# Two groups of tokens without the seven-product scheme, and router dot products that read PSUM

## The chip, the cores and the metric

The kernel runs on one core of a Trainium2 chip. The metric is the device time of the core in microseconds. A core has five engines with a queue of instructions each: TensorE (PE, matmuls; its weight loads are listed as PEld), VectorE (DVE), ScalarE (ACT), GpSimd (POOL) and SyncE (SP, which issues most DMAs here). TensorE writes its sums to PSUM, eight banks of 128 x 512 float32; the other data lie in SBUF.

## The reference

Four steps, all in float32 (`w_in` and `w_out` come as float64). For 8 x 576 = 4608 tokens:

```
attention: k, v pooled by 8 along the sequence; softmax(q k_p^T / 8) v_p, 8 heads of 64  -> x (4608 x 512)
dense:     h = x @ w_in (512 x 2048);  g = h * sigmoid(h);  x2 = g @ w_out (2048 x 512)
router:    skip = x2 @ w_skip;  logits = x2 @ w_gate (512 x 8);  e = argmax;  p = softmax(logits)[e]
experts:   tokens with skip > 0: out = x2 + p * relu(x2 @ w1[e]) @ w2[e];  the others: out = x2
```

## The kernel before

A float32 product is made of three matmuls of a rounded type (fp32r): every operand is split into a high part (a cast, on ScalarE) and a low part (operand minus high part, on VectorE or GpSimd), and high x high, high x low and low x high are summed in PSUM. So each split costs an instruction on ScalarE and one on VectorE or GpSimd.

**First product.** The tokens are taken in NS = 9 groups of 512, the 2048 hidden columns in NP = 8 pairs of two 128-column blocks. For each group and pair (number n = 8 s + p) the 2 x 2 blocks (two halves of the tokens, two of the inner dimension, two column blocks) are multiplied by Strassen and Winograd's scheme: seven block products (`product`, L433, six matmuls of 256 columns each, 42 in all) in place of eight. For this, four differences of the x quarters per group (`x_diff`, L403), seven x operands split per group in place of four (`x_hi` L415, `x_lo` L419), four sums of the weight blocks per pair, made once (`w_sums`, L238), and seven weight operands split (`w_hi` L249, `w_lo` L253). Of the seven products three are copied out of PSUM (`keep`, L445) and three more are added to these in SBUF (`total`, L449). Then silu is applied by `tanh` (L455) and `swish` (L459): in three of four blocks both operands of `swish` lie in SBUF, in the fourth one of them is PSUM. `g_store` (L464) writes g of a pair, 512 KB, to DRAM.

Ahead of that the weights are converted from float64 by integer operations: `conv_abs`, `conv_low` (ScalarE, L215, L220), `conv_mix`, `conv_or` (VectorE, L224, L229). The attention of a group (L346 to L395) runs beside the products of the group before. The operands of x lie in a ring of ten places; three of these places lie where the conversion buffers were, and can be used only when all weights are converted and summed.

**Second product and router.** 18 chunks of 256 tokens. g is loaded again (L482), split (`g_hi` L490 on ScalarE, `g_lo` L494 mostly on GpSimd) and multiplied (`mm2`, L505 to L507, 96 matmuls of 512 columns a chunk). Each of the two 128-token tiles of a chunk has its sum in a PSUM bank; the banks are 4 and 5 for even chunks, 6 and 7 for odd ones. `evac` (L514, ScalarE) copies a tile to SBUF with the factor 0.5, and from there nine dot products per tile (`dot`, L524, VectorE: a multiplication of 128 x 512 with a row of the router's weights, summed along the row) give the eight logits and the skip score. For all chunks but the last, `route_a` (L537 to L545) makes a one-hot table, two small matmuls on TensorE (`route_sum`, L552 and L553) count the tokens in front, and `route_gate` and `route_place` compute the places to which GpSimd scatters the tokens' rows (L588). These two matmuls stand in TensorE's queue amid the matmuls of the next chunk.

**Order.** Everything up to here is an operation with a cost per engine, its predecessors and the buffers it takes (`op` in `dense`). `schedule` plays the operations through by these costs, takes the engine with the earliest end where there is a choice (with the additions `FIRST`, `LATER`, `KEEP`), and writes the instructions in this order into the engines' queues. `BONUS` shifts the priority by kind and stage. `SHARED` names the VectorE operations that it lets wait for a GpSimd operation under way. At run time each queue keeps its order and waits by semaphores.

**Experts.** Token lists per expert, gathers, and two products each (L1310 to L1382), with an order written by hand.

Of the kernel before, what the change touches and what calls it, by code (L numbers as in the profile page):

```python
# [40 lines left out]
NP = NF // 2  # L41
BONUS = {
    "w": {0: -1071.7, 1: -3755.8}, "abs": {0: 73.8, 1: 863.5}, "low": {0: -1795.5, 1: 3678.9},
    "mix": {0: 475.3, 1: -8181.9}, "or": {0: 1638.6, 1: -2069}, "ws": {0: 3059.3}, "wh": {0: 450.5},
    "wl": {0: -2429.5}, "vh": {0: 5650.7}, "vl": {0: 1208.1}, "k": {0: 2715.6, 1: 3293.7, 2: -1435.3},
    "ksum": {0: 571.4}, "kput": {0: -412.3, 1: -509.7, 2: -202.1}, "v": {0: 1646.8, 1: -131.2, 2: -136.6},
    "vsum": {0: -167.3, 1: -2320.7, 2: -6962.5}, "vput": {0: -645}, "clear": {0: 1916.3},
# [15 lines left out]
    "pset": {0: 614.5}, "blank": {0: 3833.5}, "router": {0: 1355.7}, "ft": {0: -103.1}, "fi": {0: -958.4},  # L63
    "l1": {0: 2010.1}, "l2": {0: 3836.1}, "ga": {0: 4003.4}, "ti": {0: -589.9}, "tc": {0: -1820.8},
    "xp": {0: -1226.1}, "xq": {0: 3529.9}, "xr": {0: 1345}, "s1h": {0: 2372}, "s1l": {0: -3330.5},
    "s2h": {0: -4085.4}, "s2l": {0: 395.6}
# [13 lines left out]
def body(tc, const, q, k, v, w_in, w_out, w_skip, w_gate, w_r, w1, w2, out, x2d, lst, gd, base, nch):  # L80
# [3 lines left out]
    with ExitStack() as ctx:  # L84
# [155 lines left out]
        PARTS = ((0, 512), (512, 768), (768, 1280), (1280, 1792))  # L240

        def w_part(p, k):
            src = cx_t[0, 2 * p + k % 2]
            lo, hi = PARTS[k]
            return src[:, 512 - (hi - lo):512], [w[:, p * 1792 + lo:p * 1792 + hi] for w in w7]
# [153 lines left out]
        HOME = (0, 2, 3, 0, 3, 1, 2)  # L399
# [5 lines left out]
        TURN = (0, 1, 4, 5, 3, 2, 6)  # L405

        def x_op(s, k):
            n = (7 * s + TURN.index(k)) % 10
# [8 lines left out]
        def x_lo(eng, s, k):  # L417
# [3 lines left out]
        WITH = {1: (0, 0, "b"), 2: (1, 1, "a"), 3: (4, 2, "b"), 4: (2, 6, "c"), 5: (6, 3, "b"), 6: (3, 4, "b"),  # L421
                7: (5, 5, "c")}

        def product(n, m, ps):
# [5 lines left out]
            for kk in range(2):  # L430
                for a, b in ((wh, xh), (wh, xl), (wl, xh)):
                    first, end = not on and kk == 0 and b is xh and a is wh, kk == 1 and a is wl
                    nc.tensor.matmul(out=ps, lhsT=a[:, kk], rhs=b[:, kk], start=first, stop=end, skip_group_check=on)  # L433

# [164 lines left out]
        def dense():  # L599
# [4 lines left out]
            def phase(kind, a=0, *_):  # L604
                if kind in ("q", "at", "sc", "mx", "ex", "ns", "nr", "pt", "pc", "pv", "xc"):
                    return min(a // 4, 2) if a < 4 * NS - 4 else 9
                if kind in ("mm", "cp", "ad", "th", "sw", "sv", "gs"):
                    return min(a // NP, 1) if a < NN - NP else 9
                if kind in ("xd", "xh", "xl", "w", "abs", "low", "mix", "or"):
                    return min(a, 1)  # L610
# [4 lines left out]
                if kind == "dot":  # L615
                    return 0 if a // TPC < nch - 2 else 8
# [14 lines left out]
            for late in range(2):  # L631
                order = f_order(1 - late)
                for f, old in zip(order, (None, *order)):
# [3 lines left out]
                    last["cx", c] = [("vl", f)] if late else [("wh", f // 2, f % 2 + 2), ("wl", f // 2, f % 2 + 2)]  # L637
# [977 lines left out]
```

## Time and profile before

Three runs took 1408.83 to 1412.42 us, median 1409.28. The profiled execution took 1409.15 us; its span, from the first to the last instruction in the trace, is 1407.4 us, at a mean granted clock of 0.951.

| engine | busy us | share of the span | instructions |
|---|---|---|---|
| TensorE, matmuls | 1256.0 | 89% | 8068 |
| TensorE, weight loads | 1115.9 | 79% | 8068 |
| VectorE | 1034.5 | 74% | 2459 |
| ScalarE | 648.5 | 46% | 1787 |
| GpSimd | 419.5 | 30% | 401 |

Busy time is the union of an engine's instructions in the trace; those of TensorE overlap one another, so a mean duration of a matmul is longer than the distance from one to the next. [...] A wait is put down to the instruction whose end released it. The shares are means over stages that differ.

### The profile page before, as it was taken

What the parts mean: (1) busy time and instruction counts of PE and PEld (TensorE: products, weight loads), DVE (VectorE), ACT (ScalarE), POOL (GpSimd) and SP (SyncE); (2) the same over time, 40 slices, a digit from 0 to 9 for tenths busy, and PEclk for the clock granted to TensorE, in tenths of its full rate; (3) what the DMA queues carried; (4) which work ended last, traced back from release to release, by engine and by line L of the source; (5) the groups of instructions that cost most, each with busy time, mean ns of one, the idle gap of its engine ahead of it and who ended that gap; (6) DMA issues with size and microseconds to landing.
All of it is one profiled execution on the core that took longest, in us unless ns stands there. A gap on an engine that the chain in (4) does not pass through costs nothing. (4 is left out here: it accounts for less than half of the span.)

```text
span 1407.4 us, 23981 instructions
## 1 busy us (share of the span) xinstructions
PE 1256.0 (89%) x8068; PEld 1115.9 (79%) x8068; DVE 1034.5 (74%) x2459; ACT 648.5 (46%) x1787; POOL 419.5 (30%) x401
## 2 busy tenths in 40 slices
PE   3578899999999998988887888788887999999998
PEld 2468899999999997867776677677767888888887
DVE  7999978878886789696887788868787445555462
ACT  5777777767777778322221222112223344444341
POOL 3553322020200000144454444445446111112211
PEclk9689999999999999998998999989998999999999
DMA  6354434344332357633433343324341554444541
GB/s 222 121 166 132 142 139 155 129 140 160 128 123 94 125 191 258 245 105 103 137 105 105 96 136 113 105 90 138 113 165 36 179 164 162 158 154 152 197 155 46
DMA packets 83030, 196.54 MB, mean 140 GB/s; under 512 B 14599, under 2 KB 15623, under 8 KB 82752
## 3 DMA queue, kind: packets, MB, share of 16 engines
q1 hardware_dynamic: 77008, 180.28, 38.6%
q0 software_dynamic: 5872, 14.44, 3.2%
q8 instruction: 71, 1.16, 0.3%
q14 instruction: 79, 0.65, 0.1%
HBM read 175.47 MB, written 64.36 MB: 170 GB/s over the span
## 5 line engine op out<-in xcount | busy, mean ns | idle before, releaser
L524 DVE SCALAR_TENSOR_TENSOR room<-xs,room 128x512 bf16<-128x512 f32 x306 | 307.6, 1005 | 84.0 <-ACT xs L514 72.6
L433 PE MATMUL bk<-ra,w7h 128*128 128x256 f32 x1440 | 271.4, 287 | 17.0 <-ACT outs L445 10.5
L494 POOL TENSOR_TENSOR w7l<-outs,w7h 128x512 fp32r<-128x512 f32 x129 | 187.7, 1456 | 304.0 <-ACT w7h L490 302.4
L433 PEld LDWEIGHTS bk<-ra,w7h 128*128 128x128 f32 x1440 | 225.7, 193 | 21.8 <-ACT outs L445 13.6
L490 ACT CAST w7h<-outs 128x512 fp32r<-128x512 f32 x144 | 89.2, 621 | 251.6 <-PE bk L506 248.5
L433 PE MATMUL bk<-ra,w7l 128*128 128x256 f32 x720 | 204.0, 283 | 0.0
L505 PE MATMUL bk<-w7h 128*128 128x512 f32 x468 | 198.9, 425 | 5.7 <-ACT w7h L490 5.7
L506 PE MATMUL bk<-w7l,w7h 128*128 128x512 f32 x468 | 194.8, 416 | 0.0
L507 PE MATMUL bk<-w7h,w7l 128*128 128x512 f32 x468 | 194.1, 415 | 0.0
L433 PEld LDWEIGHTS bk<-ra,w7l 128*128 128x128 f32 x720 | 138.4, 192 | 0.0
L505 PEld LDWEIGHTS bk<-w7h 128*128 128x128 f32 x468 | 95.8, 205 | 26.6 <-ACT w7h L490 6.3
L449 DVE TENSOR_TENSOR outs<-outs,bk 128x256 f32<-128x256 f32 x216 | 89.5, 417 | 34.0 <-PE bk L433 14.6
L507 PEld LDWEIGHTS bk<-w7h,w7l 128*128 128x128 f32 x468 | 95.7, 204 | 22.6 <-DVE w7l L494 0.9
L506 PEld LDWEIGHTS bk<-w7l,w7h 128*128 128x128 f32 x468 | 96.6, 206 | 20.5
L433 PE MATMUL bk<-rb,w7h 128*128 128x256 f32 x576 | 109.3, 284 | 1.9 <-DVE rb L419 1.8
L1311 PE MATMUL p<-w7l,w7h 128*128 128x256 f32 x352 | 101.0, 287 | 5.9 <-DVE w7l L1296 5.9
L455 ACT ACTIVATE t<-outs 128x256 f32<-128x256 f32 x216 | 89.6, 425 | 36.1 <-DVE outs L449 26.7
L1310 PE MATMUL p<-w7h 128*128 128x256 f32 x352 | 101.2, 288 | 3.1 <-PEq L1550 1.7
L459 DVE SCALAR_TENSOR_TENSOR outs<-t,outs 128x256 f32<-128x256 f32 x216 | 93.5, 446 | 11.6 <-ACT t L455 10.2
L1382 POOL DMA_INDIRECT out_dram<-xs,room x27 | 29.0, 1074 | 244.3 <-DVE xs L1378 172.0
L1312 PE MATMUL p<-w7h,w7l 128*128 128x256 f32 x352 | 100.9, 287 | 0.0
L1314 DVE SCALAR_TENSOR_TENSOR w7l<-p,w7h 128x256 fp32r<-128x256 f32 x88 | 36.6, 423 | 86.9 <-ACT w7h L1313 68.5
(253 smaller groups left out, 2765.5 us busy)
## 6 DMA issues: line engine op xcount, KB each, us to landing
gd<-outs SPq DMA_DIRECT2D x72, 512.0 KB
outs<-gd SPq DMA_DIRECT2D x72, 512.0 KB
outs<-in_w_dram SPq DMA_DIRECT2D x56, 512.0 KB
late<-in_w_dram SPq DMA_DIRECT2D x52, 512.0 KB
room<-in_w_dram SPq DMA_DIRECT2D x48, 512.0 KB
room<-in_v_dram SPq DMA_DIRECT2D x64, 144.0 KB
room<-in_k_dram SPq DMA_DIRECT2D x32, 288.0 KB
room<-in_q_dram SPq DMA_DIRECT2D x36, 256.0 KB
```

The costliest lines, as they stand in the source:

```text
L433: nc.tensor.matmul(out=ps, lhsT=a[:, kk], rhs=b[:, kk], start=first, stop=end, skip_group_check=on)
L449: nc.vector.tensor_tensor(out=o, in0=o, in1=ps[:, 0:CH], op=ALU.add)
L455: nc.scalar.activation(out=t, in_=ps[:, 0:CH] if m == 3 else part_of(n, SUM[m]), func=ACTF.Tanh, scale=0.5)
L459: nc.vector.scalar_tensor_tensor(out=part_of(n, SUM.get(m, 3)), in0=t_t.pop((n, m)), scalar=1.0, in1=h, op0=ALU.add, op1=ALU.mult)
L494: eng.tensor_tensor(out=lo, in0=src, in1=hi.bitcast(F32), op=ALU.subtract)
L505: nc.tensor.matmul(out=ps, lhsT=gh[:, ts], rhs=vh, start=first, stop=False)
L506: nc.tensor.matmul(out=ps, lhsT=gh[:, ts], rhs=vl, start=False, stop=False)
L507: nc.tensor.matmul(out=ps, lhsT=gl[:, ts], rhs=vh, start=False, stop=end)
L524: nc.vector.scalar_tensor_tensor(out=junk, in0=x2_t[i], scalar=1.0, in1=wb[:, e * DM:e * DM + DM], op0=ALU.mult, op1=ALU.mult, accum_out=l ...
L1310: nc.tensor.matmul(out=ps, lhsT=W1h4[:, kk, m], rhs=xh[:, kk], start=(kk == 0), stop=False)
L1311: nc.tensor.matmul(out=ps, lhsT=W1h4[:, kk, m], rhs=xl[:, kk], start=False, stop=False)
L1312: nc.tensor.matmul(out=ps, lhsT=W1l4[:, kk, m], rhs=xh[:, kk], start=False, stop=(kk == KD - 1))
```

## The change

The first PLAIN = 2 groups (16 pairs) are multiplied by the plain sum: `whole`, for each of two token halves and two column blocks two block products in one PSUM bank, 12 matmuls, so 48 a pair. No differences of x, four x operands, no copies or additions out of PSUM; silu reads PSUM. The second token half of a pair comes LATE = 1 pair later, and g is stored in halves of 256 KB. The weight parts of the plain sum are split first. During the second group the weights are rebuilt from their two parts (`w_back`), their sums made (`w_sums`) and the other parts split, in five operations instead of four; the fifth takes the place of a part that the last plain products read. The groups behind run the seven products as before. In the router, `dot` reads the skip score (c = 0, the row that is listed as `dot`) from the SBUF copy as before and the other eight (now `dp`) from the PSUM tile with the factor 0.5; the PSUM bank is free when these are done, the SBUF copy when its store and the one dot are. `wc`, `ra`, `rg` and `rb` are added to `SHARED`; `dp` is not in it. All values of `BONUS` and of the engine choice are new.

```diff
+PLAIN = 2
+LATE = 1
 BONUS = {
...
         def out_slot(n):
-            n = n % 2 if n < NP else (n - NP + 2) % 4
+            n = (n - PLAIN * NP + 2) % 4
...
-        PARTS = ((0, 512), (512, 768), (768, 1280), (1280, 1792))
+        def w_back(eng, p):
+            for c in range(2):
+                o = p * 1792 + c * 512
+                t = cx_t[0, 2 * p + c] = nth("cx", cxs, 512, 4)
+                h, l = (w[:, o:o + 512].bitcast(F32) for w in w7)
+                eng.tensor_tensor(out=t, in0=h, in1=l, op=ALU.add)
+
+        PARTS = ((0, 0, 512, 0), (1, 0, 512, 512), (0, 0, 512, 1024), (1, 256, 512, 1536), (1, 0, 256, 512))
...
+        def x_slot(s, k):
+            n = 4 * s + PTURN.index(k) if s < PLAIN else 8 + 7 * (s - PLAIN) + TURN.index(k)
+            return n, (n % 7 if n < 8 else (7, 8, 9, 1, 2, 3, 4, 5, 6, 0)[(n - 8) % 10])
...
+        def half_store(n, t):
+            s, p = divmod(n, NP)
+            nc.sync.dma_start(out=gd[s][t, :, 2 * p:2 * p + 2].rearrange("p f n -> p (f n)"), in_=ot_t.pop((n, t)))
+
+        def whole(n, c, ps):
+            s, p = divmod(n, NP)
+            t, f = divmod(c, 2)
+            ps = ps[:, 0:CH]
+            for half, k in enumerate(((0, 1), (7, 2))[t]):
+                wh, wl = w_of(p, 2 * f + half)
+                xh, xl = (x.rearrange("p (k n) -> p k n", n=CH) for x in x_op(s, k))
+                for kk in range(2):
+                    for a, b in ((wh, xh), (wh, xl), (wl, xh)):
+                        first, end = half == kk == 0 and b is xh and a is wh, half == kk == 1 and a is wl
+                        nc.tensor.matmul(out=ps, lhsT=a[:, kk], rhs=b[:, kk], start=first, stop=end)
+
+        def whole_tanh(n, c, ps):
+            t = t_t[n, c] = t_p.tile([128, CH], F32, tag="t", name="t")
+            nc.scalar.activation(out=t, in_=ps[:, 0:CH], func=ACTF.Tanh, scale=0.5)
+
+        def whole_swish(n, c, ps):
+            t, f = divmod(c, 2)
+            ot_t[n, t] = outs[0][:, half_of(n, t) % 4 * 512:half_of(n, t) % 4 * 512 + 512]
+            nc.vector.scalar_tensor_tensor(out=ot_t[n, t][:, f * CH:f * CH + CH], in0=t_t.pop((n, c)), scalar=1.0,
+                                           in1=ps[:, 0:CH], op0=ALU.add, op1=ALU.mult)
...
         def dot(i, e):
             j, t = divmod(i, TPC)
-            nc.vector.scalar_tensor_tensor(out=junk, in0=x2_t[i], scalar=1.0, in1=wb[:, e * DM:e * DM + DM],
+            x, scale = (o_t[j][t], 0.5) if e else (x2_t[i], 1.0)
+            nc.vector.scalar_tensor_tensor(out=junk, in0=x, scalar=scale, in1=wb[:, e * DM:e * DM + DM],
                                            op0=ALU.mult, op1=ALU.mult, accum_out=lg_t[j][:, t, e:e + 1])
...
-                op(("ws", p), {"V": 1.36, "G": 2.76}, lambda e, p=p: w_sums(e, p), [(c, p, k) for c in ("wh", "wl") for k in range(2)])
+                op(("wc", p), {"V": 1.2, "G": 2.46}, lambda e, p=p: w_back(e, p), [("wl", p, 0), ("wl", p, 1), ("wc", p - 1) if p else ("or", 0, f_order(1)[-1])],
+                   [("cx", ("cb", p, c)) for c in range(2)])
+                op(("ws", p), {"V": 1.36, "G": 2.76}, lambda e, p=p: w_sums(e, p), [("wc", p)])
+                for k in range(5):
+                    ca, cv, cg = (0.31, 0.34, 0.69) if k > 2 else (0.52, 0.6, 1.23)
+                    d = [("ws", p) if k > 1 else ("or", 0, 2 * p + k)]
+                    if k == 4:
+                        d += [("pl", (PLAIN - 1) * NP + p, c) for c in (1, 3)]
...
+                    free = [u for n0, slot0, u in used if slot0 == slot and n0 < n][-1:]
+                    if slot > 6 and not free:
+                        free = [[("wl", p, c) for p in range(NP) for c in range(2, 5)]]
...
+                for i, cs in ((n, (0, 1)), (n - LATE, (2, 3))):
...
+                        op(prev, {"T": 1.41}, lambda e, i=i, c=c: whole(i, c, bk["pl", i, c]), deps, [B(prev)])
+                        op(("th", i, c), {"A": 0.27}, lambda e, i=i, c=c: whole_tanh(i, c, bk["pl", i, c]), [prev] + old, [("t", ("t", i, c))])
+                        op(("sw", i, c), {"V": 0.34}, lambda e, i=i, c=c: whole_swish(i, c, bk["pl", i, c]), [("th", i, c)])
+                    op(halves[-1], {"S": 1.0}, lambda e, x=halves[-1][1:]: half_store(*x), [("sw", i, c) for c in cs])
...
-                    last["o", j, t] = [("ev", j, t)]
-                    dots = [("dot", i, c) for c in range(E + 1)] if j < nch - 1 else []
-                    last["x2", i] = dots + [("st", j, t)]
+                    dots = [("dp" if c else "dot", i, c) for c in range(E + 1)] if j < nch - 1 else []
+                    last["o", j, t] = [("ev", j, t), *dots[1:]]
+                    last["x2", i] = dots[:1] + [("st", j, t)]
...
-            SHARED = ("ns", "mix", "or", "wl", "ws", "vl", "xl", "xd", "sv", "nr", "vsum", "vput", "gl", "dot", "kput")
+            SHARED = ("ns", "mix", "or", "wl", "ws", "vl", "xl", "xd", "sv", "nr", "vsum", "vput", "gl", "dot", "kput", "wc", "ra", "rg",
+                      "rb")
...
-            FIRST = {"V": 1.472, "G": 0.36099, "A": -0.83284}
-            LATER = {"V": 5.6764, "G": 0, "A": -3.582}
-            FILL, HOLD, KEEP = 575.98, 0.9, 1.6007
+            FIRST = {"V": 6.8614, "G": -6.4915, "A": 6.2963}
+            LATER = {"V": -0.60269, "G": 0, "A": -3.3824}
+            FILL, HOLD, KEEP = -724.38, 1.0, -7.6842
```

## Rows read from the trace of the kernel before

**Rows 1.** Table of stages: start:end, length, busy us and count per engine, clock, DMA.
```profile
0.00:48.40 48.40, 20.58 (x104) 16.87 (x105) 37.47 (x72) 28.11 (x87) 21.21 (x36) 0.87 0.61 198
48.40:150.10 101.70, 74.74 (x587) 67.55 (x586) 97.69 (x202) 71.87 (x243) 46.43 (x53) 0.84 0.43 141
150.10:204.50 54.40, 52.58 (x472) 50.74 (x473) 43.69 (x117) 40.07 (x143) 12.42 (x19) 1.00 0.40 139
204.50:256.50 52.00, 52.00 (x482) 50.83 (x481) 43.40 (x115) 38.46 (x141) 10.10 (x17) 1.00 0.44 148
...
584.50:606.40 21.90, 21.90 (x100) 17.94 (x98) 20.24 (x54) 6.35 (x13) 5.73 (x4) 1.00 0.43 143
...
606.40:1035.60 429.20, 361.93 (x1474) 293.23 (x1473) 340.35 (x905) 91.33 (x166) 206.15 (x154) 0.91 0.34 110
...
413.60:466.30 52.70, 52.35 (x491) 50.64 (x490) 38.23 (x109) 38.62 (x140) 0.00 (x0) 1.00 0.26 96
```

**Rows 2.** The same table for the product matmuls, L433, alone (PE, PEld), third group.
```profile
204.50:256.50 52.00, 40.91 (x338) 40.14 (x337) 1.00 0.44 148
```

**Rows 3.** Instructions of the route sum's line, L552: durations, first and last start.
```profile
L552 PE MATMUL bk<-ohb,triu x17: 169/172/183, 606.3 to 1054.3; 128*128 128x16 bf16 x17
```

**Rows 4.** Waits from 606.3 to 1054.3 us: total us, times, longest.
```profile
PE bk L552 <- DVE ohb L545: 67.3, 15, 6.2
```

**Rows 5.** Instructions in order of time, one chunk: start us, duration us, engine, line.
```profile
694.74 0.69 DVE L524 SCALAR_TENSOR_TENSOR room<-xs,room 128x512 bf16<-128x512 f32 x1 [4.41 <-ACT xs L514]
695.31 1.29 POOL L494 TENSOR_TENSOR w7l<-outs,w7h 128x512 fp32r<-128x512 f32 x1 [0.29 <-ACT w7h L490]
695.47 1.67 DVE L524 SCALAR_TENSOR_TENSOR room<-xs,room 128x512 bf16<-128x512 f32 x1
...
710.68 0.39 PE L507 MATMUL bk<-w7h,w7l 128*128 128x512 f32 x1
...
712.49 0.69 DVE L524 SCALAR_TENSOR_TENSOR room<-xs,room 128x512 bf16<-128x512 f32 x1
...
713.22 0.69 DVE L524 SCALAR_TENSOR_TENSOR room<-xs,room 128x512 bf16<-128x512 f32 x1
...
715.39 0.17 PE L552 MATMUL bk<-ohb,triu 128*128 128x16 bf16 x1 [4.32 <-DVE ohb L545]
...
716.44 0.63 PE L507 MATMUL bk<-w7h,w7l 128*128 128x512 f32 x1
716.87 0.63 PE L505 MATMUL bk<-w7h 128*128 128x512 f32 x1
...
718.80 0.39 PE L507 MATMUL bk<-w7h,w7l 128*128 128x512 f32 x1
719.03 0.39 PE L505 MATMUL bk<-w7h 128*128 128x512 f32 x1
```

**Rows 6.** Groups of instructions, 606.4 to 1035.6 us: busy us, mean ns, idle before.
```profile
L524 DVE SCALAR_TENSOR_TENSOR room<-xs,room 128x512 bf16<-128x512 f32 x270 | 276.9, 1025 | 78.2 <-ACT xs L514 68.0 <-DVE room L524 0.5
```

**Rows 7.** Instructions in order of time in the first group, GpSimd and VectorE.
```profile
84.96 1.47 POOL L253 TENSOR_TENSOR w7l<-cxs,w7h 128x512 fp32r<-128x512 f32 x1
85.20 0.41 DVE L449 TENSOR_TENSOR outs<-outs,bk 128x256 f32<-128x256 f32 x1
...
86.38 1.83 DVE L459 SCALAR_TENSOR_TENSOR outs<-t,outs 128x256 f32<-128x256 f32 x2
86.39 1.53 POOL L308 TENSOR_TENSOR room<-room 72x512 f32<-72x512 f32 x1
```

**Rows 8.** Groups of VectorE's instructions, 413.6 to 466.3 us.
```profile
L459 DVE SCALAR_TENSOR_TENSOR outs<-t,outs 128x256 f32<-128x256 f32 x24 | 9.8, 422 | 2.3 <-ACT t L455 2.0
...
L459 DVE SCALAR_TENSOR_TENSOR outs<-t,bk 128x256 f32<-128x256 f32 x8 | 3.3, 412 | 0.0
```

**Rows 9.** Groups of VectorE's instructions in the first group, 48.4 to 150 us.
```profile
L238 DVE TENSOR_TENSOR cxs<-cxs 128x256 f32<-128x256 f32 x20 | 11.2, 559 | 0.5
L253 DVE TENSOR_TENSOR w7l<-cxs,w7h 128x512 fp32r<-128x512 f32 x13 | 11.1, 864 | 0.0
```

More of the change, by code (lines that the diff above doesn't have):

```diff
@@ L398, in body @@
         DIFF = {3: (0, 1, 0), 5: (1, 3, 1), 4: (3, 3, 0), 6: (2, 2, 3)}
-        HOME = (0, 2, 3, 0, 3, 1, 2)
+        HOME = (0, 2, 3, 0, 3, 1, 2, 1)
         def x_diff(eng, k):
@@ L636, in dense @@
                     last["sg", c] = [("or", *c)]
-                    last["cx", c] = [("vl", f)] if late else [("wh", f // 2, f % 2 + 2), ("wl", f // 2, f % 2 + 2)]
+                    last["cx", c] = [("vl", f)] if late else [("wh", f // 2, f % 2), ("wl", f // 2, f % 2)]
                     op(("w", *c), {"S": 1.95}, lambda e, c=c: load_w(*c), gone,
@@ new lines, in dense @@
+                for k in PTURN if s < PLAIN else range(7):
+                    n, slot = x_slot(s, k)
+                    free = [u for n0, slot0, u in used if slot0 == slot and n0 < n][-1:]
+                    if slot > 6 and not free:
+                        free = [[("wl", p, c) for p in range(NP) for c in range(2, 5)]]
+                    free = free[0] if free else []
+                    if s < PLAIN:
+                        used.append((n, slot, [("pl", s * NP + NP - 1, c) for c in ((0, 1) if k < 2 else (2, 3))]))
+                    else:
+                        used.append((n, slot, [("mm", s * NP + NP - 1, m) for m in WITH if WITH[m][1] == k]))
+                    used.sort(key=lambda x: x[0])
@@ L783, in dense @@
                     op(("xh", s, k), {"A": 0.52}, lambda e, s=s, k=k: x_hi(s, k), needs[k] + free)
                     op(("xl", s, k), {"V": 0.6, "G": 1.23}, lambda e, s=s, k=k: x_lo(e, s, k), [("xh", s, k)])
-            prev = None
-            for n in range(NN + 1):
+            prev, halves = None, []
+            for n in range(PLAIN * NP + LATE):
+                for i, cs in ((n, (0, 1)), (n - LATE, (2, 3))):
+                    if not 0 <= i < PLAIN * NP:
+                        continue
+                    s, p = divmod(i, NP)
+                    old = halves[-4:-3]
+                    halves.append(("gs", i, cs[0] // 2))
+                    for c in cs:
+                        deps = [prev, *[("xl", s, k) for k in ((0, 1), (7, 2))[c // 2]], s == 0 and ("wl", p, c % 2)]
+                        last["pl", i, c], last["t", i, c] = [("sw", i, c)], [("sw", i, c)]
+                        prev = ("pl", i, c)
+                        op(prev, {"T": 1.41}, lambda e, i=i, c=c: whole(i, c, bk["pl", i, c]), deps, [B(prev)])
+                        op(("th", i, c), {"A": 0.27}, lambda e, i=i, c=c: whole_tanh(i, c, bk["pl", i, c]), [prev] + old, [("t", ("t", i, c))])
+                        op(("sw", i, c), {"V": 0.34}, lambda e, i=i, c=c: whole_swish(i, c, bk["pl", i, c]), [("th", i, c)])
+                    op(halves[-1], {"S": 1.0}, lambda e, x=halves[-1][1:]: half_store(*x), [("sw", i, c) for c in cs])
@@ L788, in dense, with held @@
+            def held(n):
+                at = n - PLAIN * NP - 2
+                return [("gs", n - 4)] if at > 1 else halves[2 * at - 4:2 * at - 2 or None] if at >= 0 else []
+            for n in range(PLAIN * NP, NN + 1):
                 for d, m in ((0, 1), (0, 2), (1, 3), (0, 6), (1, 4), (0, 7), (0, 5)):
                     i = n - d
-                    if i < 0 or i == NN:
+                    if i < PLAIN * NP or i == NN:
                         continue
@@ L805, in dense @@
                     if m in (1, 6, 5):
-                        old = i - (2 if i < NP else 4)
                         op(("cp", i, m), {"A": 0.31}, lambda e, i=i, m=m, key=key: keep(i, m, bk[key]),
-                           [prev, m == 1 and old >= 0 and ("gs", old)])
+                           [prev] + (m == 1) * held(i))
                     if m in SUM:
@@ L819, in dense, with stored @@
                     op(("gs", n), {"S": 1.95}, lambda e, n=n: g_store(n), [("sw", n, 3)] + [("sv", n, m) for m in (2, 4, 7)])
+            def stored(j, a):
+                ns = [j // 2 * NP + 2 * a + c for c in range(2)]
+                return [("gs", n, j % 2) if n < PLAIN * NP else ("gs", n) for n in ns]
             for j in range(nch):
@@ L825, in dense @@
                     op(("ld", j, a), {"S": 1.95}, lambda e, j=j, a=a: g_load(j, a),
-                       old + [("gs", j // 2 * NP + 2 * a + c) for c in range(2)])
+                       old + stored(j, a))
                 for q, a in enumerate(blocks(j)):
@@ L845, in dense @@
                     op(("st", j, t), {"S": 1.95}, lambda e, i=i: store(i), [("ev", j, t)])
-                    for c in range(E + 1):
-                        if j < nch - 1:
-                            op(("dot", i, c), {"V": 0.72}, lambda e, i=i, c=c: dot(i, c), [("ev", j, t), ("router",)])
+                    for c, name in enumerate(dots):
+                        op(name, {"V": 0.73}, lambda e, i=i, c=c: dot(i, c), [dots[0] if c else ("ev", j, t), ("router",)])
                 if j == nch - 1:
@@ L852, in dense @@
                 op(("ra", j), {"V": 1.44}, lambda e, j=j: route_a(j),
-                   [("dot", TPC * j + t, c) for t in range(TPC) for c in range(E + 1)])
+                   [("dp" if c else "dot", TPC * j + t, c) for t in range(TPC) for c in range(E + 1)])
                 op(("rp", j), {"T": 0.06}, lambda e, j=j: route_sum(j, bk["rp", j]), [("ra", j)], [B(("rp", j), range(4))])
```

71 lines of the change are left out of this document (36 added, 35 removed), and 31 rows, old and new, of the table BONUS.

## Prediction

> **What bounds the kernel now.** I read the table of stages first, then the waits of the longest slow stage, then one chunk of it instruction by instruction, and last the durations of like instructions in other stages. The run has three stretches: the first dense product with the attention, the second dense product with the router, and the experts.
>
> In the table of stages TensorE is busy all of a full group, 52.00 of 52.00 us for eight pairs of 256 hidden columns plus the attention of the next group, at full granted clock. But the first group takes 101.7 us, the second 54.4, and the first product starts only at 48.4 us; there VectorE is busy 97.69 of 101.7 us and TensorE's granted clock is 0.84 [rows 1]. The row of the products alone confirms that this stretch is one group: 338 matmuls, where eight pairs of seven products of six make 336 [rows 2]. So the start, to 204.5 us, is VectorE's, and the seven groups behind it are TensorE's.
>
> The second dense product is neither engine's: from 606.4 to 1035.6 us TensorE is busy 362 of 429 us, VectorE 340, at clock 0.91. One chunk, 584.5 to 606.4, shows the pace without a stall: 21.90 us, all of it TensorE's, at clock 1.00 [rows 1]. The matmuls that sum the routes are a tick mark, one per chunk: 17 of them from 606.3 to 1054.3, so 448.0 / 16 = 28.0 us a chunk [rows 3]. That is 6.1 us a chunk over the pace, 16 x 6.1 = 97.6 us in all. The waits name it: TensorE stood 67.3 us in 15 waits before that matmul, for VectorE's one-hot table [rows 4].
>
> One chunk shows why. The 18 router dot products start at 694.74 us. One that runs alone takes 0.69 us and the next starts 0.73 later (712.49, 713.22). One that meets GpSimd's subtraction (1.29 us from 695.31) takes 1.67 us. TensorE finishes its product work ahead of the route sum at 710.68 + 0.23 = 710.91, and stands till 715.39. [...]
>
> **The dots from PSUM.** Eight of nine per tile, 16 of 18 per chunk, now read one operand from PSUM. The mean of a dot is 1.025 us there, against 0.69 alone [rows 5, 6]. What decides is whether a VectorE instruction with one PSUM operand still meets GpSimd. The early stage answers it. GpSimd runs L253 from 84.96 to 86.43; inside it VectorE's addition with a PSUM operand takes 0.41 us, no more than the swish of that size needs from PSUM where GpSimd does nothing, 0.41. The next GpSimd instruction starts at 86.39, and two swishes with both operands in SBUF need 1.83 us for what is 0.42 each alone [rows 1, 7, 8]. So I cost a PSUM dot at 0.73 us from start to start. 18 dots: 18 x 0.73 = 13.1 us from 694.74, so 707.9. The route arithmetic up to the matmul takes from the end of the last dot's slot, 713.22 + 0.73 = 713.95, to 715.39, 1.4 us, which makes 709.3, 1.6 us before TensorE comes to it. The two dots that still read SBUF can each meet GpSimd, 2 x 0.98 us late: 711.3, or 0.4 us of stall at the worst. The route arithmetic, now beside a GpSimd that no longer starves, may meet it once more (1 us). I take 0.6 us a chunk for stall and misplacement together, so 22.0 + 0.6 = 22.6 us a chunk and a gain of 16 x (28.0 - 22.6) = 86 us. Bounds: all of the 97.6 us, or nothing (and below nothing, as the last rival). Cover: VectorE was busy 340.35 us in this stretch of 15.3 chunks, 276.9 of it dots, so 4.1 us a chunk go to everything else [rows 1, 6]; 13.1 + 4.1 + 2 for the two meetings is 19.2, below 21.9 us, so TensorE bounds. The PSUM banks are held until the last dot, some 14 us longer; the bank pair is wanted again only two chunks on, 22 us after. Loads and stores move 110 GB/s here and would need 28.0 / 22.6 of it, 136 GB/s, less than the 198 of the first 48 us [rows 1].
>
> [...] The trace has the two forms of the swish side by side with GpSimd idle: 412 ns from PSUM, 422 from SBUF [rows 8]. By that I add nothing.
>
> **The plain sum in the first two groups.** TensorE: 48 matmuls of 256 columns a pair in place of 42, so 384 a group. At 40.91 / 338 = 0.121 us each [rows 2] a group's products take 46.5 us instead of 40.9; with the 52.0 - 40.9 = 11.1 us that attention has beside them, 57.6 us. From 48.4 us on two groups end at 163.6.
>
> VectorE, both groups together: gone are 3 additions x 16 pairs x 0.41 = 19.7 us, and of the x side 8 differences and 6 splits at the 0.86 us of a 128x512 tensor operation in this stage, 12.0 us. New are 16 additions that rebuild the weights from their two halves, 16 x 0.86 = 13.8, and 8 more splits of 256 columns at 0.56, 4.5 us [rows 8, 9]. Net -13.4 us of the 37.47 + 97.69 + 43.69 = 178.9 that VectorE spends up to 204.5 [rows 1]; 165.5 us at its present share of 0.96 end at 172. The sums of the weights (4 x 0.56 a pair) and three of the splits aren't saved but moved from the first group to the second; there VectorE was busy 43.69 of 54.4 us, and GpSimd, busy 12.42, can take a part [rows 1]. ScalarE loses 48 copies and 6 casts and gains 8 short ones; it was busy 71.87 of 101.7 us and does not bound.
>
> Moved past queues: the 512 KB store of a pair becomes two of 256 KB, so 16 more issues on SP, each of which can hold a weight load behind it until its swish is done. The stores go out one pair later for the second tile. I cost that at nothing; DMA moved 141 GB/s in the first group and weights are wanted faster, but 198 was reached before [rows 1].
>
> A new wait: the last weight part overwrites what the last plain products read, and the third group's first operand lies in the place of the conversion buffers, so cast, subtraction, cast, subtraction stand in a row between the last plain product and the next: about 0.4 + 0.6 + 0.6 + 0.7 and the hand-overs, an estimate of 4 us, and the attention of the next group can fill part of it. Queued behind it on TensorE is everything.
>
> Sum: between TensorE's 163.6 and VectorE's 172, plus 4 for that wait and 2 for two engines that both near their limit, 178 us in place of 204.5: -26 us. Bounds: -40 (TensorE alone bounds), and +16 (VectorE's saving is lost in the second group, and the 11.2 us of added matmuls and the wait stand).
>
> Everything else (seven full groups, the expert stage) I cost at nothing: the same instructions under the same bound. The whole planned order is new, which the rows cannot price.
>
> **Sum.** The profiled execution took 1409.15 us, 0.13 below the median 1409.28. 1409.15 - 86 - 26 = 1297.
>
> **Rivals.**
> Only the second product gains: the start gives its saving back, because the second group becomes VectorE's with 8 x (2 x 0.86 + 4 x 0.56 + 0.86 + 2 x 0.56) = 47.5 us of weight work beside its own. For it: VectorE is at 0.80 there already. Against it: the first group loses nearly as much. 1409 - 86 = 1323; with the whole +16, 1339.
> Only the start gains: dots from PSUM meet GpSimd as before, or another wait, such as GpSimd's low halves, takes the stall's place at the same 28 us. Against it: L449 inside L253 [rows 7], and GpSimd's waits are for ScalarE, which waits for TensorE. 1409 - 26 = 1383.
> Slower: a 128x512 dot from PSUM is itself slow while TensorE writes PSUM on every cycle, place VectorE between the tile's copy and the route sum. It decides from 1.025 + 26 / (16 x 16) = 1.13 us a dot on. At 1.18, half way between the short and the long dot, 16 x 16 x (1.18 - 1.025) = 40 us more: 1409 + 40 - 26 = 1423. Against it: every PSUM form in the rows is as short as its SBUF form, but at 256 columns only.
>
> **Chances.** Forecast 0.74 (own range 1270 to 1316), only the second product 0.15, only the start 0.07, slower 0.03, the rest 0.01 for no change. The range reaches from both gains in full, 1409 - 97.6 - 40 = 1271, to the first rival and most of its loss, 1335; I set 1268 to 1335. Within 0.3% is about what a measurement of this kernel can't tell from no change: 0.01. Slower 0.03, faster 0.96.
>
> **What would show it.** Right: the dots' mean falls to about 0.7 us with GpSimd's subtractions beside them; the wait of the route sum all but goes; route sums lie 22 to 23 us apart and the clock of that stretch is near 1.00. At the start, the third group's first product is near 178 us with a gap of a few us ahead of it. Wrong: dots above 0.9 us; a chunk still near 28 us with another releaser; the third group at 204 us or later; VectorE full and TensorE waiting in the second group.

## The result and the profile after

The changed kernel took 1283.66 us (median of 4 runs, 1282.66 to 1284.93), the kernel before 1409.37 beside it: a ratio of 0.9104, interval 0.9089 to 0.9120, some 126 us. The forecast was 1297, range 1268 to 1335. In the repeat of the changed kernel, the last of the experiments, one of six runs took 4255.83 us, and the numbers given for that repeat are those of the other five.

The span fell by 124.2 us, from 1407.4 to 1283.2. It is cut at the first matmul of the third group, at the first and the last matmul of the second product, and at the end:

| stretch | before, us | after, us | difference |
|---|---|---|---|
| start, two groups | 204.5 | 190.4 | -14.1 |
| groups three to nine | 350.8 | 354.0 | +3.2 |
| second product, router | 505.8 | 398.3 | -107.5 |
| experts | 346.4 | 340.4 | -6.0 |

The table of stages of the changed kernel, which answers to [rows 1]: start:end, length, busy us (and count) of TensorE, its weight loads, VectorE, ScalarE and GpSimd, granted clock (as a share of full speed), DMA share and GB/s. The first row is the lead-in up to the first product, the next two are the plain groups, the fourth the third group; the last three are the first chunk of the second product, the second chunk, and the 15 chunks behind them.
```profile
0.00:51.20 51.20, 26.60 (x136) 21.58 (x137) 37.93 (x74) 28.25 (x98) 11.05 (x24) 0.97 0.60 198
51.20:120.10 68.90, 65.47 (x570) 63.10 (x569) 64.46 (x140) 49.87 (x164) 19.07 (x23) 0.95 0.56 179
120.10:190.40 70.30, 64.20 (x554) 61.14 (x553) 62.61 (x146) 39.52 (x151) 29.49 (x40) 0.95 0.41 131
190.40:247.20 56.80, 54.17 (x480) 51.43 (x481) 45.98 (x119) 40.85 (x147) 11.11 (x17) 1.00 0.40 130
...
544.40:569.20 24.80, 23.84 (x97) 19.15 (x98) 16.11 (x27) 12.12 (x23) 0.00 (x0) 0.93 0.95 329
569.20:591.00 21.80, 21.80 (x99) 17.89 (x98) 18.91 (x58) 6.58 (x12) 0.00 (x0) 1.00 0.44 145
591.00:919.80 328.80, 328.80 (x1474) 270.05 (x1474) 273.44 (x964) 92.82 (x166) 114.38 (x95) 1.00 0.45 143
```
Two things are to be seen. In the last row TensorE is busy all of 328.80 us at clock 1.00, where it had 361.93 of 429.20 at 0.91: the second product is now TensorE's from its second chunk on. In the start the 102 and 54 us of the first two groups have become 69 and 70, and neither engine quite fills either of them.

The route sum's line in the changed kernel, the tick mark of [rows 3] (count, shortest, median and longest ns, first and last start), and what that line still waited for from 591.0 to 919.8 us, against [rows 4] (total us, times, longest):
```profile
L597 PE MATMUL bk<-ohb,triu x17: 182/183/184, 590.9 to 936.1; 128*128 128x16 bf16 x17
```
```profile
PEld L597 <- issue: 4.2, 16, 0.3
```
The ticks span 345.2 us where they spanned 448.0. The last row of the table holds 15 chunks (1474 matmuls) in 328.80 us, 21.9 us each; before, the same 1474 took 429.20 us [rows 1], 28.6 each. No wait of TensorE's matmuls for another engine is left in these chunks; 0.3 us a chunk of queue issue before the weight load is all.

VectorE's groups in the same 328.8 us (busy us, mean ns, then the idle time before them), against [rows 6]:
```profile
L569 DVE SCALAR_TENSOR_TENSOR room<-bk,room 128x512 bf16<-128x512 f32 x240 | 165.9, 691 | 8.3
L538 DVE TENSOR_TENSOR w7l<-outs,w7h 128x512 fp32r<-128x512 f32 x59 | 40.8, 691 | 15.7 <-ACT w7h L534 15.3 <-issue 0.3
L569 DVE SCALAR_TENSOR_TENSOR room<-xs,room 128x512 bf16<-128x512 f32 x30 | 20.7, 689 | 21.1 <-ACT xs L558 20.9
```
A dot takes 691 ns from PSUM and 689 from SBUF. The middle row was not forecast: 59 of the low halves of g (`g_lo`), which had nearly all been GpSimd's, are made by VectorE here. In the whole run GpSimd made 129 of the 144 before and makes 64 now; the new constants of the engine choice did that (with other constants, in an experiment below, GpSimd makes 134).

One chunk in order of time (start, duration, engine, line), against [rows 5]:
```profile
704.11 1.28 POOL L538 TENSOR_TENSOR w7l<-outs,w7h 128x512 fp32r<-128x512 f32 x1 [3.42 <-ACT w7h L534]
...
704.23 0.69 DVE L569 SCALAR_TENSOR_TENSOR room<-bk,room 128x512 bf16<-128x512 f32 x1
...
704.96 0.69 DVE L569 SCALAR_TENSOR_TENSOR room<-bk,room 128x512 bf16<-128x512 f32 x1
...
715.70 0.17 DVE L590 CAST ohb<-oh 128x16 bf16<-128x16 f32 x1
...
716.98 0.18 PE L597 MATMUL bk<-ohb,triu 128*128 128x16 bf16 x1
```
GpSimd's subtraction runs from 704.11 to 705.39, and the two dots beside it take 0.69 us and follow each other at 0.73. The one-hot table is ready at 715.87; TensorE comes to the route sum at 716.98. Where TensorE stood for 4.3 us [rows 5], VectorE is now 1.1 us ahead.

Of the start, four views say why it gained only 14 us. First VectorE's groups in the second plain group, 120.1 to 190.4 us, the three costliest:
```profile
L241 DVE TENSOR_TENSOR cxs<-cxs 128x256 f32<-128x256 f32 x24 | 14.7, 612 | 0.6
L476 DVE SCALAR_TENSOR_TENSOR outs<-t,bk 128x256 f32<-128x256 f32 x31 | 12.4, 412 | 5.8 <-ACT t L471 5.8
L248 DVE TENSOR_TENSOR cxs<-w7h,w7l 128x512 f32<-128x512 f32 x12 | 9.9, 865 | 0.0
```
Then a stretch of that group in order of time:
```profile
164.55 3.18 DVE L241 TENSOR_TENSOR cxs<-cxs 128x256 f32<-128x256 f32 x4
...
165.39 1.59 POOL L298 TENSOR_TENSOR room<-room 128x288 f32<-128x288 f32 x2
...
167.64 0.74 DVE L476 SCALAR_TENSOR_TENSOR outs<-t,bk 128x256 f32<-128x256 f32 x2
...
168.11 2.19 PE L356 MATMUL bk<-room 128*64 128x144 f32 x16 [2.80 <-DVE outs L476]
```
All that TensorE's matmuls waited for in the second group (us in total, times, longest):
```profile
PE bk L356 <- DVE outs L476: 2.8, 1, 2.8
PE bk L386 <- DVE outs L476: 1.8, 3, 0.9
PE bk L467 <- DVE outs L476: 0.2, 1, 0.2
```
And the boundary of the second and the third group on TensorE:
```profile
186.81 1.07 PE L386 MATMUL bk<-ident,room 128*72 128x128 f32 x8 [0.59 <-DVE outs L476]
187.81 1.25 PE L356 MATMUL bk<-room 128*128 128x144 f32 x8
190.45 0.50 PE L447 MATMUL bk<-rb,w7h 128*128 128x256 f32 x2 [1.39 <-DVE outs L476]
```
Four sums of weights (L241) with GpSimd beside them take 3.18 us on VectorE, two `swish` (L476) stand behind them in its queue, and TensorE waits 2.80 us for a PSUM bank that these free. All five waits of the group, 4.8 us together, end with a `swish`: what holds TensorE is VectorE's order of work, not one missing operand. The boundary itself costs two waits, one of these five (0.59 us) and one of 1.39 us.

### The profile page after: what moved, and what is told of

Read it like the earlier page. It is cut to its first block, busy times and chain, and to the rows that moved or that the text cites. A ratio compares the mean times of both kernels' runs of the same rounds, so it can differ in the third digit from the quotient of the medians.

```text
span 1283.2 us, 24162 instructions
## 1 busy us (share of the span) xinstructions
PE 1231.3 (96%) x8164; PEld 1103.6 (86%) x8164; DVE 946.9 (74%) x2506; ACT 633.3 (49%) x1741; POOL 288.5 (22%) x312
## 5 line engine op out<-in xcount | busy, mean ns | idle before, releaser
L447 PE MATMUL bk<-ra,w7h 128*128 128x256 f32 x1088 | 199.5, 283 | 1.1 <-ACT outs L489 0.7
L569 DVE SCALAR_TENSOR_TENSOR room<-bk,room 128x512 bf16<-128x512 f32 x272 | 188.0, 691 | 9.3
L447 PEld LDWEIGHTS bk<-ra,w7h 128*128 128x128 f32 x1088 | 166.8, 189 | 2.8 <-ACT outs L489 1.3
L447 PE MATMUL bk<-ra,w7l 128*128 128x256 f32 x544 | 152.5, 280 | 0.0
L538 POOL TENSOR_TENSOR w7l<-outs,w7h 128x512 fp32r<-128x512 f32 x64 | 82.3, 1290 | 102.9 <-ACT w7h L534 102.9
L447 PEld LDWEIGHTS bk<-ra,w7l 128*128 128x128 f32 x544 | 102.4, 188 | 0.0
L633 POOL DMA_INDIRECT lst<-row,du x36 | 40.5, 1125 | 266.6 <-DVE du L630 226.8
L1397 ACT ACTIVATE w7h<-p 128x256 fp32r<-128x256 f32 x88 | 33.5, 383 | 130.0 <-PE p L1396 130.0
L370 ACT ACTIVATE room<-bk,mx 128x72 f32<-128x72 f32 x288 | 88.8, 329 | 16.0 <-DVE mx L362 14.4
L467 PE MATMUL bk<-ra,w7h 128*128 128x256 f32 x512 | 96.0, 290 | 0.2 <-DVE outs L476 0.2
L447 PE MATMUL bk<-rb,w7h 128*128 128x256 f32 x480 | 91.3, 285 | 4.2 <-ACT outs L489 1.9
```

Source lines behind the costliest of these rows:

```text
L370: nc.scalar.activation(out=P_t[i][:, HP * g + h], in_=ps[:, h], func=ACTF.Exp, scale=esc, bias=mx[:, h], accum_out=sm_t[i][:, HP * g + h])
L538: eng.tensor_tensor(out=lo, in0=src, in1=hi.bitcast(F32), op=ALU.subtract)
L569: nc.vector.scalar_tensor_tensor(out=junk, in0=x, scalar=scale, in1=wb[:, e * DM:e * DM + DM], op0=ALU.mult, op1=ALU.mult, accum_out=lg_t[ ...
```

## The experiments

The account of the prediction for the second product: a dot with one operand in PSUM no longer meets GpSimd, and that alone is the gain. Its rival: the low halves that moved from GpSimd to VectorE removed the collisions, and PSUM has little to do with it. For the start: VectorE still bounds it; rivals are TensorE, the late second token half, and the hand-over at the boundary. A stage's times below are from the profiled execution of each kernel; ratios are to the kernel before, beside it on the same chip.

**The dots alone.** The kernel before, with eight of nine dots read out of PSUM and the PSUM bank held until they are done; start and engine choice as before, and the planned cost of a dot 0.73 us for 0.72. The line that reads x (the code that frees the bank and the SBUF copy is left out here):
```diff
-  in0=x2_t[i], scalar=1.0
+  x, scale = (o_t[j][t], 0.5) if e else (x2_t[i], 1.0)
+  in0=x, scalar=scale
```


> The kernel before with the dots from PSUM alone; first groups, priorities and engine choice as before. Theory A: dots 0.7 us, chunks near 22 us from the 28.0 of before, a gain of 85 to 105 us: 1304 to 1324 us. Theory B: most low halves stay on GpSimd and the order is the old one, so a gain under 40 us: over 1369 us.


Measured 1306.0 us, ratio 0.9268 [0.9229, 0.9306]: -103 us. The dots' group and the route sum's line of this kernel:
```profile
L525 DVE SCALAR_TENSOR_TENSOR room<-bk,room 128x512 bf16<-128x512 f32 x272 | 187.9, 691 | 9.3
```
```profile
L553 PE MATMUL bk<-ohb,triu x17: 169/183/184, 604.5 to 950.3; 128*128 128x16 bf16 x17
```
691 ns a dot and 345.8 us from the first tick to the last, with 129 of the low halves on GpSimd as before. The account holds and the rival is not needed.

**The dots back in SBUF.** The changed kernel, all nine dots from the SBUF copy; the bank is free again when the tile is copied (that code is left out here).
```diff
-  x, scale = (o_t[j][t], 0.5) if e else (x2_t[i], 1.0)
+  x, scale = x2_t[i], 1.0
```


> The changed kernel with all nine dots reading the SBUF copy again; costs, order rules and engine choice stay those of the changed kernel. Theory A (the PSUM operand keeps the dots out of GpSimd's way): about four low halves a chunk still run on GpSimd, each makes a dot about 1 us longer; dots' mean 0.85 to 1.0 us, chunks of 24 to 28 us where the changed kernel has 21.9, total 1315 to 1380 us. Theory B (the gain comes from moving over half of the low halves from GpSimd to VectorE and from the new order): chunks stay under 22.7 us, total under 1297 us.


Measured 1348.58, ratio 0.9564 [0.9523, 0.9604]: 65 us of the gain gone. Its dots, and TensorE's wait for the one-hot table (591 to 1000 us):
```profile
L569 DVE SCALAR_TENSOR_TENSOR room<-xs,room 128x512 bf16<-128x512 f32 x306 | 276.8, 905 | 33.0 <-ACT xs L558 23.7
```
```profile
PE bk L597 <- DVE ohb L590: 46.8, 16, 5.0
```
The dots are at 905 ns and the stall is back, but smaller than [rows 4] has it, since only 64 low halves are left on GpSimd. The dots' operand apart, TensorE, ScalarE and GpSimd run the same instructions in the same order as in the changed kernel, and so does VectorE but for 13 neighbouring pairs of small instructions (L613, L622), so another order did not make the difference.

**The low halves back on GpSimd.** The changed kernel with constants of the engine choice that give GpSimd 134 of the 144 low halves.
```diff
-  FIRST = {"V": 6.8614, "G": -6.4915, "A": 6.2963}
+  FIRST = {"V": -0.60269, "G": 0, "A": -3.3824}
-  LATER = {"V": -0.60269, "G": 0, "A": -3.3824}
-  FILL, HOLD, KEEP = -724.38, 1.0, -7.6842
+  LATER = {"V": 5.6764, "G": 0, "A": -3.3824}
+  FILL, HOLD, KEEP = 540.0, 1.0, 0.0
```


> The changed kernel with dots from PSUM, but the low halves of the second product priced off VectorE as in the kernel before, so that nearly all run on GpSimd. Theory A: dots stay at 0.69 us beside a GpSimd twice as busy, chunks about 22 us, total 1276 to 1294 us. Theory B: the stall before the route sum comes back, chunks of 25 us or more, total over 1330 us.


Measured 1287.12, ratio 0.9126 [0.9088, 0.9163], which can't be told from the changed kernel's. Its two groups:
```profile
L569 DVE SCALAR_TENSOR_TENSOR room<-bk,room 128x512 bf16<-128x512 f32 x272 | 187.9, 691 | 9.4
```
```profile
L538 POOL TENSOR_TENSOR w7l<-outs,w7h 128x512 fp32r<-128x512 f32 x134 | 174.6, 1304 | 247.2 <-ACT w7h L534 246.8
```
Twice as many GpSimd subtractions, and no dot from PSUM is longer.

**The start alone.** The two edits above together, so that of the change only the start is left.


> The changed kernel with both of the second product's parts undone: nine dots from SBUF and the low halves priced onto GpSimd as before, so the plain sum of the first groups stands alone. If the parts add as measured so far (third group's first product 190 us for 204.5, and some 4 us at the change to the second product), chunks are back at 27 to 29 us and the total is 1385 to 1398 us, a gain of 12 to 24 us. Rival (the start's gain was an effect of the new order as a whole): total 1400 us or more.


Measured 1391.03, ratio 0.9883 [0.9860, 0.9905]: -17 us, small but clear of 1. Its dots and the wait (591 to 1040 us):
```profile
L569 DVE SCALAR_TENSOR_TENSOR room<-xs,room 128x512 bf16<-128x512 f32 x306 | 310.7, 1015 | 87.7 <-ACT xs L558 76.5
```
```profile
PE bk L597 <- DVE ohb L590: 71.7, 17, 8.1
```
So the parts add up: -103 for the dots and -17 for the start are -120 of some -126. The low halves are worth some 42 to 45 us where dots read SBUF (1391.0 to 1348.6, or 0.9883 to 0.9564 by the ratios), and nothing that can be measured where they read PSUM. The rival names a real remedy, a second one for the same collision, which the first one makes idle.

**Without the weight sums.** The changed kernel with the instructions of `w_sums` left out, so the groups from the third on multiply wrong weights and the tokens are routed otherwise; what is compared is the start.
```diff
-  lambda e, p=p: w_sums(e, p)
+  lambda e, p=p: None
```


> The changed kernel without the four sums of weight blocks per pair (their instructions left out, so the products of the later groups use unsummed blocks; order and all else the same). Takes some 14 to 18 us of work off VectorE in the second group. Theory V (the second group, 70.3 us, is VectorE's, with the silu queued behind weight work): second group 60 to 64 us, total 1273 to 1278 us. Rival (the group is paced by TensorE's own 58 us, the attention chain and ScalarE): under 3 us, total 1280 to 1284 us.


The third group began at 180.4, 10.0 us earlier. The whole run, 1258.22 (ratio 0.8913), is no measure, for its expert stage is 13.5 us shorter with other tokens. Its second group, in the columns of the first table:
```profile
118.90:180.40 61.50, 61.14 (x555) 58.98 (x553) 52.51 (x122) 39.16 (x151) 29.76 (x40) 1.00 0.48 154
```
Ten us less on VectorE (52.5 for 62.6), and TensorE is busy 61.14 of 61.50 us at clock 1.00. With these 14.7 us of sums gone, the group is TensorE's. With them it is 8.8 us longer: TensorE is idle for 6.1 us of it instead of 0.4, and as many matmuls keep it busy for 3.1 us more, at clock 0.95 for 1.00.

**The weight work on GpSimd.** Twice: `w_back` on GpSimd alone, and `w_sums` on GpSimd alone.
```diff
-  op(("wc", p), {"V": 1.2, "G": 2.46}
+  op(("wc", p), {"G": 2.46}
```


> The changed kernel with the rebuilding of the weights (two additions a pair) allowed on GpSimd alone: 16 us off VectorE in the second group, some 22 us onto GpSimd. Theory V (VectorE's time in the second group sets its length): third group's first product at 180 to 186 us, total 1274 to 1280 us. Rival (longer GpSimd work holds VectorE's instructions with two SBUF operands, which are most of that group's weight work): third group at 188 us or later, total 1282 to 1292 us.


```diff
-  op(("ws", p), {"V": 1.36, "G": 2.76}
+  op(("ws", p), {"G": 2.76}
```


> The changed kernel with the four weight sums of a pair allowed on GpSimd alone: 18 us off VectorE in the second group, some 22 us onto GpSimd, in a chain of four for each pair. Theory V: third group at 180 to 187 us, total 1273 to 1281 us. Rival: third group at 188 us or later, total 1282 to 1295 us.


Measured 1291.6 (0.9181 [0.9157, 0.9206]) and 1288.99 (0.9162 [0.9139, 0.9184]): slower than the changed kernel. The third group began earlier, at 186.6 and 187.3, but its first pair took 15.46 and 12.38 us instead of 7.18, and the second product began at 547.9 and 545.7 instead of 544.5. TensorE at the boundary, with `w_back` on GpSimd:
```profile
186.58 0.35 PE L447 MATMUL bk<-rb,w7h 128*128 128x256 f32 x1 [3.66 <-POOL room L298]
...
193.72 0.58 PE L447 MATMUL bk<-rb,w7h 128*128 128x256 f32 x1 [3.92 <-ACT rb L429]
```
GpSimd is now late with the attention's own work (L298), and the x operands of the third group come after it. What was won is more than given back at the boundary. And less was won than was moved. `w_back` had been 15.5 us of VectorE and `w_sums` 18.1, but VectorE's busy time up to the third group fell only from 165.0 to 161.0 and 157.3 us, for other instructions of VectorE became longer beside a GpSimd that does more. The 28 scalings of the row maximum (4 columns each) went from 7.1 to 10.9 us in the first of the two runs, the 28 of the softmax sum from 7.0 to 9.7 in the second. Those that overlap no work of GpSimd took 173 ns at most, as before; what grew is the number and the time of the others. The rival of the first expectation had named this. Both totals lie in the rivals' ranges, but both starts of the third group lie between the ranges of the two theories.

**The second token half at once.** The changed kernel with no delay between a pair's halves.
```diff
-LATE = 1
+LATE = 0
```


> The changed kernel with LATE = 0: both token halves of a pair right after each other, so the very first pairs need all four tiles of the group's attention. First product of the first group's second half waits for tiles 2 and 3: first group longer by 2 to 8 us, total 1284 to 1294 us. If the attention is ahead anyway: within 2 us of the changed kernel.


Measured 1285.03, ratio 0.9125 [0.9101, 0.9150]: no difference from the changed kernel that these intervals show. The first product began at 45.5 us, nearly 6 earlier, and the third group at 192.3, 2 later. In this start, TensorE's beginning earlier did not bring the end forward.

**Taking small work off VectorE.** The changed kernel without the scaling of the softmax sum, a VectorE instruction on 4 columns per half tile; the factor goes into ScalarE's copy of x, and the added 1e-9 is left out. The planned order is the same.
```diff
-  nc.vector.tensor_scalar(out=sm, in0=sm, scalar1=1e-9, scalar2=float(POOL), op0=ALU.add, op1=ALU.mult)
-  nc.scalar.copy(out=x5[...], in_=ps...)
+  nc.scalar.activation(out=x5[...], in_=ps..., func=ACTF.Copy, scale=1.0 / POOL)
```


> The changed kernel in the same planned order, without the small scaling of the softmax sums (72 instructions of VectorE on 4 columns, 0.17 us alone and 0.58 beside GpSimd; the factor 1/8 goes into ScalarE's copy of x instead, the 1e-9 is left out as it vanishes beside sums of at least 1). Theory V (VectorE's time in the first two groups sets their length): 28 of them lie before the third group, 7 us of VectorE; third group's first product at 183 to 187 us, total 1275 to 1280 us. Rival (the wait between second and third group or the attention chain sets it): third group within 2 us of 190, total 1281 to 1285 us.


Measured 1278.15 (1276.24 to 1279.97), ratio 0.9075 [0.9052, 0.9099]. The third group began at 184.3 (-6.1), the second product at 537.1 (-7.4). What was taken out, in the changed kernel's start (0 to 190.4 us; count, shortest, median and longest ns):
```profile
L375 DVE TENSOR_SCALAR sm<-sm x28: 155/164/1264, 16.3 to 184.8; 128x4 f32<-128x4 f32 x28
```
These 28 are 7.0 us of VectorE, and the third group came 6.1 us earlier.

Two steps further: the same edit with the planner told of the shorter operation (0.18 us instead of 0.3), and this with the scaling of the row maximum moved to ScalarE as well.
```diff
-  op(("ns", i, g), {"V": 0.3}
+  op(("ns", i, g), {"V": 0.18}
```


> The same edit, and the planner told of the shorter cost, so the order of everything is new. Theory V: total 1272 to 1281 us; if a new order is worth more than the edit, anything from 1272 to 1290 us.


```diff
-  nc.vector.tensor_scalar(out=mx, in0=mx, scalar1=-esc, scalar2=None, op0=ALU.mult)
+  nc.scalar.activation(out=mx, in_=mx, func=ACTF.Copy, scale=-esc)
```


> As the run before, and the scaling of the row maxima moved from VectorE to ScalarE (72 more instructions of 4 columns, 0.17 us alone and 0.49 beside GpSimd on VectorE, about 0.2 us on ScalarE). Another 7 us off VectorE before the third group, and ScalarE, busy 49.9 of 68.9 us in the first group, takes 2 to 3 us there. Theory V: third group at 178 to 184 us, total 1268 to 1277 us. Rival: ScalarE or the attention chain becomes the bound, total 1278 us or more.


Measured 1281.17 (0.9093 [0.9069, 0.9116]) and 1286.99 (0.9137 [0.9115, 0.9159]). The third group began at 183.4 and 185.9. The last is a miss: VectorE has 154 us of work up to 190.4 us instead of 165, yet the third group begins only 4.6 us earlier than in the changed kernel, its first pair takes 10.37 us, and the second product starts at 547.6. With the costs changed the planner wrote another order, and that order lost what the engine had won. In the run before it the first pair took 11.0 us.

**The changed kernel again**, to have a second interval for it.


> The changed kernel itself once more, in five rounds, to set its ratio beside that of the version without the scaling of the softmax sums (0.9075). If that version is faster by its 5.5 us, this ratio is 0.910 to 0.9125, total 1281 to 1286 us; if the difference came from chip or round, 0.907 to 0.909, total 1276 to 1281 us.


Measured 1284.46 (1282.84 to 1287.40), ratio 0.9121 [0.9109, 0.9134]. The kernel without the softmax scaling, 0.9075 [0.9052, 0.9099], lies below this interval, and overlaps the first one of the changed kernel, 0.9089 to 0.9120, by 0.001. By the ratios it is 4 to 6.5 us faster, the fastest kernel here that computes the whole but for the 1e-9.

## Why the prediction was right, and where it was not

**What bounds the kernel.** Right. The second product was held up by VectorE's one-hot table and went to TensorE's pace when the dots became short; the dots alone did it, and with the order kept and the dots put back, 65 us were lost again.

**The dots.** 0.73 us from start to start was right to the hundredth. Right too that a PSUM operand takes the dot out of GpSimd's way: of the changed kernel's dots from PSUM, 170 overlap a GpSimd tensor operation, and they all take 690 to 693 ns; before, 185 of 306 did, at a mean of 1210 ns and 3220 at the longest, and those beside no GpSimd work took 692. Beside GpSimd, then, dots with two SBUF inputs take 1210 ns on average, and dots with one, at 690 to 693, lose nothing; by what mechanism, no run was made to say. Adding nothing for the read from PSUM was right as well: 691 ns from PSUM against 689 from SBUF in the changed kernel.

The term was mis-sized. The forecast was 86 us; from the first tick to the last the gain is 448.0 - 345.2 = 102.8. Two steps gave too little. The 0.6 us a chunk put in for stall was none: the two SBUF dots a chunk meet GpSimd hardly at all (689 ns), TensorE was never kept waiting, and a chunk took 21.9 us where 22.6 was forecast, some 11 us in all. The rest is in "448.0 / 16 = 28.0 us a chunk". Counted in both traces, the first tick stands behind 2.00 chunks' worth of the second product's matmuls, the next ones behind 2.81 and 3.75, and the last behind 17.75, so the 16 intervals hold 15.75 chunks. That is 28.4 us a chunk before and 21.9 after, the 21.90 us that the prediction took as the pace; the whole loss was 448.0 - 15.75 x 21.9 = 103 us, not the 97.6 of the upper bound, and all of it was won. The first chunk, 29.3 us before and 24.7 after, was not in the sum. It takes 24.8 us with the start alone and 29.3 with the dots alone, so this gain comes from the new start and order. With it nearly all of the 107.5 is accounted for.

**The start.** The mechanism was right, the size was not: -14 us for -26, within the bounds of -40 and +16. VectorE's work was worked out rightly, 165.5 us against 37.93 + 64.46 + 62.61 = 165.0. The step that failed is "at its present share of 0.96 end at 172". The 0.96 belongs to the first group alone; [rows 1] have VectorE busy 37.47 of 48.40 us in the lead-in before it, 0.77, and the change leaves that stretch as it is. Over the whole start its share was 178.9 / 204.5 = 0.875, and it was 165.0 / 190.4 = 0.867 after. 165.5 / 0.875 would have been 189, an estimate made afterwards. With the lead-in kept apart, 48.4 + (165.5 - 37.5) / 0.96 gives 182; the rest is a lead-in that became 2.8 us longer and a share of 0.91 in the two groups, 127.1 us of 139.2, where 0.96 was taken. That VectorE's work holds up this end, experiments bear out: without the weight sums the third group came 10.0 us earlier and the group became TensorE's, and 7.0 us less of tiny instructions brought 6.1. It is not the amount of work alone: with 15.5, 18.1 and 14.1 us of instructions taken off VectorE in other ways, the third group came 3.9, 3.2 and 4.6 us earlier.

TensorE's 57.6 us a group was reached by neither group: its matmuls of the plain products took 49.6 and 48.2 us of busy time instead of 46.5, at clock 0.95, and it was busy 65.5 of 68.9 and 64.2 of 70.3. Even the group that TensorE bounds, the one without the weight sums, took 61.5 us at clock 1.00. The first product began later, at 51.3 us instead of 48.4; the run without the delay shows that this does not set the end. That GpSimd "can take a part" of the weight work was right as a statement of room and would have been wrong as a remedy. The new wait at the boundary, put at 4 us, was 2.0 in the two waits shown. Behind it the third group took 56.8 us instead of 52.0 [rows 1], TensorE idle for 2.6 of them and busy 2.2 longer; groups three to nine together took 3.2 us more.

**Costed at nothing.** The engine choice of the low halves was overlooked; it changed nothing that can be measured once the dots read PSUM. The experts took 6.0 us less with the same instructions; the kernels here that compute the whole lie between 339 and 346, and no run was made to say why. That stays open.

So 1297 was 13 us too high: the gain was put about 22 us too low for the second product and 12 too high for the start, and the other two stretches together gave less than 3. That two misses of opposite sign left 13 is luck.

**The rivals.** "Only the second product gains" had its reason right, for the second group did become 15.9 us longer with the weight work on VectorE, but the first became 32.8 us shorter. "Only the start gains" and "slower" fell with 691 ns a dot.

## What to carry to other kernels

Where VectorE and GpSimd both work from SBUF, look at the spread of one instruction's durations (683 to 3220 ns for a dot in the kernel before), not at the busy share; reading one operand straight from PSUM, before the copy, took the collision away here without moving any work (691 ns a dot in the kernel with the dots alone), and moving the GpSimd work instead was then no longer needed. When a bound is worked out as work divided by a share, take the share of the same stretch, its lead-in included. And work taken off the bounding engine is won only if the order still brings the next stage's first operands in time: look at the first pair behind a boundary (15.46 and 12.38 us here instead of 7.18), not only at the time of the boundary. Work moved to GpSimd can also lengthen what stays on VectorE, as the weight work did (28 small scalings from 7.1 to 10.9 us, 28 others from 7.0 to 9.7).

## What the runs showed of the hardware

**The collision costs GpSimd too.** The subtraction for the low halves before, and in the changed kernel (the latter as the page has it):
```profile
L494 POOL TENSOR_TENSOR w7l<-outs,w7h 128x512 fp32r<-128x512 f32 x129 | 187.7, 1456 | 304.0 <-ACT w7h L490 302.4 <-DVE gw L561 1.3
```
```profile
L538 POOL TENSOR_TENSOR w7l<-outs,w7h 128x512 fp32r<-128x512 f32 x64 | 82.3, 1290 | 102.9 <-ACT w7h L534 102.9
```
Beside dots from SBUF it takes 1456, 1455 and 1442 ns on average in three kernels, with 129, 64 and 134 subtractions; beside dots from PSUM 1290, 1304 and 1306 in three others, with 64, 134 and 129. It goes with the dots' operand, not with the number of subtractions. In the kernel before, the 96 subtractions that overlap a dot take 1511 ns on average, the 33 that overlap none 1295.

**Four columns are held up by GpSimd too.** The softmax scaling above, on 4 columns, takes 164 ns as a rule and 1264 at the longest; the mean of the 28 in the start is 250 ns. Of all 72 in the run, the 13 that overlap GpSimd's work take 579 ns on average, and none of the others more than 173. An operation that seems too small to count was worth some 6 us of a stage that VectorE bounds.

**With the stall gone, the clock was higher as well.** TensorE stood 67.3 us in 15 chunks [rows 4], 4.5 us a chunk; the 15 chunks of the table became 100.4 us shorter (429.20 to 328.80), 6.7 each. The other 2.2 us a chunk are TensorE's own busy time, 361.93 and 328.80 us for the same 1474 matmuls, and went with the granted clock of that stretch, 0.91 before and 1.00 after. Behind the wait shown in [rows 5] the matmuls start 0.43 us apart (716.44, 716.87), with a granted clock of 0.50 from 715.40 to 718.40 us, and then 0.23 apart (718.80, 719.03), with a clock of 1.00 from 719.40 to 722.00.
